# Attention scores on 64x64 quarters of TensorE, with new ranks, in an attention and mixture-of-experts kernel

## The chip, the cores and the metric

The kernel runs on one core of a Trainium2 chip, in one launch. The metric is the device time of the whole launch in microseconds; less is better. TensorE multiplies, VectorE, ScalarE and GpSimd do the rest, and SyncE issues most transfers. A product on TensorE reads both operands from SBUF and writes PSUM, which has eight banks of 128 partitions x 512 float32.

## The reference

Attention over 8 batches, 8 heads, 576 positions and 64 numbers a head, causal with a window of 128 keys and a bias by distance; then a mixture of 8 experts, of which each of the 4608 tokens takes two.

```python
scores = scale * np.matmul(q, k.transpose(0, 1, 3, 2))
bias = slopes[:, None, None] * (-np.abs(rel).astype(np.float32))[None, :, :]
mask = (rel >= 0) & (rel < window)                       # window = 128
scores = np.where(mask, scores + bias[None], -1000000000.0)
attn = softmax(scores)                                   # written out in full in the source
x = np.matmul(attn, v)                                   # to rows of 512 = 8 heads x 64
logits = x @ w_gate
noisy_logits = logits + np.log1p(np.exp(x @ w_noise)) * noise
top2 = np.argpartition(-noisy_logits, 2, axis=1)[:, :2]  # softmax weights over the two
for e in range(8):
    for k in range(2):
        mask = top2[:, k] == e
        h = np.maximum(x[mask] @ w1[e], 0.0)             # 512 -> 1024
        out[mask] += top2_w[mask, k, None] * (h @ w2[e]) # 1024 -> 512
```

## The kernel before

**Pairs and groups.** Work of attention goes by pairs of heads: 32 pairs (8 batches x 4), `k` in the code. One tile `qk` holds a pair: head 0 on partitions 0 to 63, head 1 on 64 to 127; in its columns the queries (`QW` = 640: 512, then the last 64 of head 0 and of head 1 side by side, with zeros on the other head's partitions) and then the 576 keys. The 576 queries are five blocks, four of 128 and one of 64. A `unit` is a pair and one of three groups of blocks: (0, 1), (2, 3), and the last block alone, which two pairs share; that is 80 units.

**A unit's stages.** `scores` (L498) multiplies a block of 128 queries with its 128 or 256 keys, for each head on its own 64 rows of the array, into that head's PSUM bank `s[h]`; `scores_of_last` (L513) does the last block of one pair, both heads in one full product with 192 keys, into `s[z]` for pair `z` of two. VectorE brings the 128 keys of each query's window together (`copy_predicated`, L524 and L532), adds the bias and takes the largest (L516); ScalarE takes the exponential (L540, L546); TensorE transposes (L553); ScalarE or VectorE copies the result out of PSUM (`evac`, L267 or L271); GpSimd cuts it at the diagonal (L573, L574); TensorE multiplies with the values (`weigh` L589, `weigh_last` L598) on two column halves. `rows`, `row_major` (L734, L737) and `gate` (L759, four strips of 32 columns; L770, L775) make token rows and gate logits of a batch, `route(b)` chooses the experts and writes the list of tokens (L875 and others).

**The experts.** Three blocks of expert 0 (384, 384 and 256 tokens, from the first 4, 6 and 7 batches) can start while attention runs; all others come in a second wave. `ups` (L1272) and `downs` (L1316, L1321) are float16 products in three passes, of weights and tokens split into a high and a low half (L1208 and L1244 make the low halves).

**What sets the order.** The program writes out its instructions in the order of a planner that runs at build time (class `Order`). Each piece of work is a coroutine that asks for an engine with a cost in microseconds and a rank (`pe`, `act`, `dve`, `pool`, `move`; `either` may go to ScalarE or VectorE, with an extra rank for VectorE). An engine that is free takes the ready piece of the lowest rank; TensorE prefers, within `NEAR` ranks, a piece of the same array mode (`like`) and is charged `SWITCH` where the mode changes. Ranks are the position `t` in the list of units plus constants: `STAGE` for the stages of a unit, `GATE`, `ROUTE`, `SCATTER` for a batch, `FFN0`, `FFN1`, `WEIGHTS`, `TOKENS`, `SIZES` for the experts, `LATE` for the engine choice. Costs and ranks only set the order; on the chip every engine runs its list in order and waits on semaphores. Tiles go round in rings (`qkr` 5, `pr` 5, `ptr` 4, two pairs of banks for scores in `sb`, two banks each in `tb` and `ob`).

Of the kernel before, what the change touches and what calls it, by code (L numbers as in the profile page):

```python
# [18 lines left out]
B, H, S, D = 8, 8, 576, 64  # L19
N, DM, E, F = B * S, H * D, 8, 1024  # L20
W = 128
NQ = 5
NP = H // 2
QW = 512 + 128
GROUPS = ((0, 1), (2, 3), (4,))
NF = 1
FIRST = ((0, 384, 4), (384, 384, 6), (768, 256, 7))
# [10 lines left out]
NTR = 512  # L38
NPAD = N + NTR
BLOCKS = tuple(((FROWS, c - FROWS),) if z < NF else ((0, 512), (512, 384), (896, c - 896)) for z, c in enumerate(CAPS))  # L40
ZERO, EMPTY = 61.9, -14
LOAD = -47.8
VALUES = 56.6
GATE = (-11.1, 47.4, 137.6, -25.3)
ROUTE = (1.0, 14.0, 40.1, 47.7)
SCATTER = (60.8, -1065.1, -1061.7, -1053.1, -38.3)
FFN0, FFN1 = 165.6, 267.3
WEIGHTS = (94.7, 86.4)
TOKENS = 101.2
STAGE = (-8.0, 5.7, 9.8, -7.2, -2.2, 32.3, 14.3, -20.1)  # L50
MIDDLE = 101.0
RESULT = -68.3
SIZES = (71.1, 72.1, 977.3)
SOON = 22.3
TIGHT = (1, 5, 7)
QUICK = (5, 7)
LATE = (-6.5, -40.7, 45.4, 103.9, -13.4, -112.7, 32.0, -155.9, 105.8, -25.4, 51.6, -29.7)
LAG = 0.2
TURN, MARGIN, LATE_BY = (1.4, 0.3), 1.0, 1.0
PACE, READ_BY, AHEAD = 4.0, 2.0, 16  # L60
HELD = 3
# [166 lines left out]
def attention_moe(ctx: ExitStack, tc: tile.TileContext, qk_, v, w_gate, w_noise, noise, w1, w2,  # L228
                  out, xs, slots, eye):
    nc = tc.nc  # L230
# [5 lines left out]
    bank = [psum.tile([128, 512], F32, name=f"bank{i}") for i in range(8)]  # L236
# [5 lines left out]
    order = Order()  # L242
# [5 lines left out]
    def pe(us, rank, emit, join=True, mode="full"):  # L248
        return Op((("PE", us, rank),), emit, join, mode)
# [51 lines left out]
    rel4, relc4 = scratch[1][:, 0:W], scratch[1][:, W:2 * W]  # L301
# [39 lines left out]
    def slope(h):  # L341
        return -8.0 * 2.0 ** -(h + 1)

    def masks():
        def window(out_, rel_):

            nc.vector.tensor_scalar(out_, rel_, 0.0, float(W), op0=OP.is_lt, op1=OP.mult)
            nc.vector.tensor_add(out_, out_, rel_)

        def full():  # L350
            nc.vector.tensor_scalar(own_key, rel, 0.0, None, op0=OP.is_ge)
            window(rel2[:, 0], rel)
            nc.vector.tensor_scalar(rel2[:, 1], rel, 0.0, 2.0 ** 40, op0=OP.is_lt, op1=OP.mult)
            nc.vector.tensor_add(rel2[:, 1], rel2[:, 1], rel)

        def halves():
            nc.vector.tensor_scalar(own_key4, rel4[:, 0:64], 0.0, None, op0=OP.is_ge)
            window(relc4, rel4)

        def bias_of(e, h):  # L360
            copy(e, bias[:, :, h], rel2, scale=slope(h))
            part = slice(h % 2 * 64, h % 2 * 64 + 64)
            copy(e, bias4[part, h // 2], relc4[part], scale=slope(h))

        yield dve(0.14, -40, lambda: nc.vector.tensor_scalar(ident, rel, 0.0, None, op0=OP.is_equal))
        yield dve(0.14, -40, lambda: nc.vector.tensor_scalar(before, rel, 0.0, None, op0=OP.is_lt))
        yield dve(1.0, -40, full)
        yield dve(0.6, -40, halves)
        for g in range(NP):
            for h in (2 * g, 2 * g + 1):  # L370
                yield either(0.56, 0.37, -20 + 5 * g, LATE[9], lambda e, h=h: bias_of(e, h))
            mark(biased[g])
# [118 lines left out]
    def scores(k, blocks, s):  # L491
        qk = qks[k]
        for z, i in enumerate(blocks):
            k0, c = (i - 1) * 128 if i else 0, width(i)
            o = place_of(blocks, z)
            for h in range(2):
                half = slice(h * D, h * D + D)
                nc.tensor.matmul(s[h][:, o:o + c], qk[half, i * 128:i * 128 + 128], qk[half, QW + k0:QW + k0 + c],  # L498
                                 start=True, stop=True)

    def width(i):
        return (128, 256, 256, 256, 192)[i]
# [7 lines left out]
    def scores_of_last(k, s):  # L510
        for z in range(2):
            qk = qks[k + z]
            nc.tensor.matmul(s[z][:, 0:192], qk[:, 512:QW], qk[:, QW + S - 192:QW + S], start=True, stop=True)  # L513

    def biased_and_largest(o, i, by, m):
        nc.vector.tensor_tensor_reduce(out=o, in0=i, in1=by, scale=-0.125, scalar=3.0e38, op0=OP.add, op1=OP.min, accum_out=m)  # L516
# [11 lines left out]
                biased_and_largest(p[:, z, h], s[h][:, o:o + W], bias[:, int(i == 0), 2 * g + h], nm[:, z, h:h + 1])  # L528

    def top_of_last(k, s, p, nm):  # L530
        for z in range(2):
            nc.vector.copy_predicated(s[z][:, 0:64], own_key4.bitcast(U32), s[z][:, W:W + 64])  # L532
        for z in range(2):
            biased_and_largest(p[:, z, 0], s[z][:, 0:W], bias4[:, (k + z) % NP], nm[:, z, 0:1])

    def soft(g, blocks, p, nm, den):
        for z, i in enumerate(blocks):
# [3 lines left out]
                                     accum_out=den[:, i, 2 * g + h:2 * g + h + 1])  # L541

    def soft_of_last(g, p, nm, den):
        for z in range(2):
            pv = p[:, z, 0]
            nc.scalar.activation(pv, pv, AF.Exp, bias=nm[:, z, 0:1], scale=-1.0,  # L546
                                 accum_out=den[:, 0, 2 * g + 2 * z:2 * g + 2 * z + 1])

    def trans(p, t, nh):
        for z in range(2):  # L550
# [4 lines left out]
    def evac(e, blocks, t, pt):  # L555

        if blocks == (4,):
            copy(e, pt[:, :, 0], t[:, 0:2 * W].rearrange("p (z c) -> p z c", z=2))
        else:
            copy(e, pt[:, :, 0:2] if blocks[0] == 0 else pt[:, :, 0:4:2], t.rearrange("p (h z c) -> p h z c", h=2, z=2))  # L560

    def split(blocks, pt):

        if blocks == (4,):
            a, b = (pt[:, :, x].rearrange("p z (h c) -> p z h c", h=2) for x in (0, 1))
            pattern = [[0, 2], [0, 2], [1, 64]]
# [24 lines left out]
    def weigh_last(k, pt, o):  # L591

        t = values_[k // 2]
        for z in range(2):
            for at, kb in ((0, 3), (1, 4)):
                for h in range(2):
                    half, hh = slice(h * D, h * D + D), (2 * z + h) * D
                    nc.tensor.matmul(o[half, z * D:z * D + D], t[:, kb, hh:hh + D], pt[:, z, at, half], start=at == 0, stop=at == 1)  # L598

    over, attended, seated = Event(n + B + B * NQ), Event(PAIRS + PAIRS // 2), Event(n)  # L600
    stored = [Event(NQ) for _ in range(B)]
# [10 lines left out]
    def unit(u):  # L612
# [5 lines left out]
        if last:  # L618
# [4 lines left out]
        yield biased[g + last]  # L623
        s = yield (sb, r0)
        mark(seated)
        yield pe((0.77, 0.98, 0.53)[gr], r0, lambda: scores_of_last(k, s) if last else scores(k, blocks, s),
                 mode="full" if last else "rows")
        for z in range(k, k + 1 + last):
            left[z] -= 1
            if not left[z]:  # L630
# [63 lines left out]
    def rows(b, last, t):  # L694

        yield filled[b, last]
        blocks, den = ((0, 1, 2, 3), (4,))[last], dens[b, last]
        nr, nz = 64 if last else 128, len(blocks)
        rank = t - GATE[kind(b)]

        def sums():
            if last:
                nc.vector.tensor_scalar(den[0:64, 0, 1:H:2], den[64:128, 0, 0:H:2], 1e-9, None, op0=OP.add)
                nc.vector.tensor_scalar(den[0:64, 0, 0:H:2], den[0:64, 0, 0:H:2], 1e-9, None, op0=OP.add)
# [867 lines left out]
    steps = [(blk, f) for blk in first + second for f in range(8)]  # L1572
    ranks = ranks1 + [1000 + s for s in range(8 * len(second))]

    nc.gpsimd.memset(ones, 1.0)
    nc.gpsimd.memset(one, 1.0)
    nc.gpsimd.iota(rel, pattern=[[-1, W]], base=0, channel_multiplier=1, allow_small_or_imprecise_dtypes=True)
# [1 line left out]
        nc.gpsimd.iota(rel4[z * 64:z * 64 + 64], pattern=[[-1, W]], base=0, channel_multiplier=1,  # L1579
                       allow_small_or_imprecise_dtypes=True)  # L1580
    nothing = nc.gpsimd.to_reg(0.0)
    order.busy["POOL"], order.busy["DVE"], order.busy["ACT"] = 2.5, 1.5, 1.9
    order.at(2.5, lambda: order.dispatch("POOL"))
    order.at(1.5, lambda: order.dispatch("DVE"))
# [101 lines left out]
```

## Time and profile before

| what | value |
|---|---|
| time of the runs | 1040.87 us median of 3 (1038.19 to 1041.65) |
| span of the profiled execution, first to last instruction | 1039.9 us |
| mean granted TensorE clock | 0.990 of 2.4 GHz |
| busy: TensorE, its weight loads, VectorE, ScalarE, GpSimd | 1006.7, 613.2, 684.7, 440.4, 367.3 us |
| first expert matmul starts | 231.1 us |
| last matmul ends | about 1030 us |

The profile names its own time as the span; no separate time of that execution is given, so the span stands for it, 0.9 us below the median of the runs. PE is TensorE, PEld its weight loads, DVE VectorE, ACT ScalarE, POOL GpSimd, SP SyncE. Busy time is the union of an engine's instructions. A line L498 is that line of the kernel. In a row, `out<-in` names the tile written and the tiles read, without buffer numbers; `64*128 64x256` is a stationary tile of 64 rows and 128 columns with a moving tile of 64 rows and 256 columns. A float32 product appears as two records.

### The profile page before, as it was taken

What the parts mean: (1) busy time and instruction counts of PE and PEld (TensorE: products, weight loads), DVE (VectorE), ACT (ScalarE), POOL (GpSimd) and SP (SyncE); (2) the same over time, 40 slices, a digit from 0 to 9 for tenths busy, and PEclk for the clock granted to TensorE, in tenths of its full rate; (3) what the DMA queues carried; (4) which work ended last, traced back from release to release, by engine and by line L of the source; (5) the groups of instructions that cost most, each with busy time, mean ns of one, the idle gap of its engine ahead of it and who ended that gap; (6) DMA issues with size and microseconds to landing.
All of it is one profiled execution on the core that took longest, in us unless ns stands there. A gap on an engine that the chain in (4) does not pass through costs nothing. (4 is left out here: it accounts for less than half of the span.)

```text
span 1039.9 us, 20426 instructions
## 1 busy us (share of the span) xinstructions
PE 1006.7 (97%) x6952; PEld 613.2 (59%) x6952; DVE 684.7 (66%) x2410; ACT 440.4 (42%) x1218; POOL 367.3 (35%) x572
## 2 busy tenths in 40 slices
PE   8998999989999999999999999999999999999996
PEld 6776766656557645654574457456644754584454
DVE  8988999997756857744777566467636834773311
ACT  8976887762222524332342344134313421442211
POOL 4356686664633203331232233143203320332202
PEclk9999999989999999999999999999999999999998
DMA  9856989835399879893997489859957794864223
GB/s 345 297 173 209 310 306 307 291 72 142 59 251 188 203 200 177 134 207 107 182 205 173 73 175 187 203 78 171 208 156 106 152 189 153 172 132 68 37 24 49
DMA packets 193338, 178.61 MB, mean 172 GB/s; under 512 B 104080, under 2 KB 147376, under 8 KB 193232
## 3 DMA queue, kind: packets, MB, share of 16 engines
q1 hardware_dynamic: 175888, 138.35, 49.2%
q0 software_dynamic: 17344, 38.94, 23.9%
q8 instruction: 55, 0.90, 0.4%
q14 instruction: 51, 0.42, 0.1%
HBM read 117.29 MB, written 40.71 MB: 152 GB/s over the span
## 5 line engine op out<-in xcount | busy, mean ns | idle before, releaser
L1405 POOL DMA_INDIRECT out_dram<-yo,ix x69 | 110.4, 1600 | 497.5 <-ACT yo L267 448.3
L1292 ACT ACTIVATE hh<-bank 128x384 f16<-128x384 f32 (+9 forms) x192 | 92.9, 484 | 449.4 <-PE bank L1272 442.5
L1307 DVE SCALAR_TENSOR_TENSOR hl<-bank,hh 128x384 f16<-128x384 f32 (+9 forms) x200 | 108.8, 545 | 255.9 <-ACT hh L1292 255.0
L1316 PEld LDWEIGHTS <-hh 128*128 128x128 f16 (+1 forms) x944 | 92.2, 98 | 100.2
L1272 PE MATMUL bank<-xh,w1hb 128*128 128x512 f16 (+8 forms) x384 | 127.0, 331 | 0.4 <-DMA xh<-th 0.4
L1272 PE MATMUL bank<-xh,w1lb 128*128 128x512 f16 (+8 forms) x384 | 127.1, 331 | 0.0
L1272 PE MATMUL bank<-xl,w1hb 128*128 128x512 f16 (+8 forms) x384 | 126.9, 330 | 0.1
L1272 PEld LDWEIGHTS <-w1ha 128*128 128x128 f16 x832 | 80.5, 98 | 48.8
L1272 PEld LDWEIGHTS <-w1hb 128*128 128x128 f16 x768 | 75.3, 98 | 55.5 <-issue 2.3
L1272 PE MATMUL bank<-xh,w1ha 128*128 128x384 f16 (+8 forms) x320 | 102.0, 319 | 0.0
L1272 PE MATMUL bank<-xh,w1la 128*128 128x384 f16 (+8 forms) x320 | 102.0, 319 | 0.0
L1272 PE MATMUL bank<-xl,w1ha 128*128 128x384 f16 (+8 forms) x320 | 102.0, 319 | 0.0
L540 ACT ACTIVATE p<-p,nm 128x128 f32<-128x128 f32 x256 | 99.0, 392 | 5.6 <-DVE nm L516 5.6
L1316 PE MATMUL bank<-w2ha,hl 128*128 128x512 f16 x244 | 92.5, 379 | 0.3 <-DVE hl L1307 0.3
L1316 PE MATMUL bank<-w2ha,hh 128*128 128x512 f16 x244 | 92.5, 379 | 0.0
L1316 PE MATMUL bank<-w2la,hh 128*128 128x512 f16 x244 | 92.5, 379 | 0.0
L1316 PE MATMUL bank<-w2hb,hl 128*128 128x512 f16 x228 | 86.4, 379 | 0.7 <-DVE hl L1307 0.7
L1316 PE MATMUL bank<-w2hb,hh 128*128 128x512 f16 x228 | 86.4, 379 | 0.0
L1316 PE MATMUL bank<-w2lb,hh 128*128 128x512 f16 x228 | 86.4, 379 | 0.0
L1219 POOL DMA_INDIRECT xg<-xs_dram,ix x69 | 73.8, 1070 | 32.4 <-issue 14.8
L1316 PEld LDWEIGHTS <-hl 128*128 128x128 f16 x472 | 46.4, 98 | 57.5 <-DVE hl L1307 2.4
L498 PE MATMUL bank<-qk 64*128 64x256 f32 (+1 forms) x512 | 67.1, 385 | 7.0 <-DMA qk<-in_qk_dram 4.6
(250 smaller groups left out, 2036.3 us busy)
## 6 DMA issues: line engine op xcount, KB each, us to landing
raw<-in_w_dram SPq DMA_DIRECT2D x144, 256.0 KB, 4.8
mraw<-in_w_dram SPq DMA_DIRECT2D x56, 512.0 KB, 4.1
qk<-in_qk_dram SPq DMA_DIRECT2D x32, 608.0 KB, 5.3
vraw<-in_v_dram SPq DMA_DIRECT2D x16, 640.0 KB, 6.6
out_dram<-xg SPq DMA_DIRECT2D x10, 1024.0 KB, 7.6
xs_dram<-x SPq DMA_DIRECT2D x32, 256.0 KB, 5.4
xg<-xs_dram,ix POOLq DMA_INDIRECT x69, 5.8
xh<-th SPq DMA_TRANSPOSE x69, 6.0
```

The costliest lines, as they stand in the source:

```text
L498: nc.tensor.matmul(s[h][:, o:o + c], qk[half, i * 128:i * 128 + 128], qk[half, QW + k0:QW + k0 + c], start=True, stop=True)
L540: nc.scalar.activation(pv, pv, AF.Exp, bias=nm[:, z, h:h + 1], scale=-1.0, accum_out=den[:, i, 2 * g + h:2 * g + h + 1])
L1219: yield pool(1.04, rank, lambda: nc.gpsimd.indirect_dma_start(out=xg[0:r], out_offset=None, in_=xs[0:blk.rows], in_offset=bass.IndirectOff ...
L1272: nc.tensor.matmul(t[:, 0:blk.n], wp[:, c], x[:, c, 0:blk.n], start=c == 0 and z == 0, stop=c == 3 and z == 2)
L1292: nc.scalar.activation(o, i, AF.Relu)
L1307: yield dve(0.07 + c * 0.00104, rank - MIDDLE, lambda: nc.vector.scalar_tensor_tensor(hl[:, 0:c], t[:, 0:c], 0.0, hh[:, 0:c], op0=OP.max, ...
L1316: nc.tensor.matmul(blk.y[j][0:r], h[:, cs], wp, start=f == 0 and m == 0, stop=f == 7 and m == 2)
L1405: ins = nc.gpsimd.indirect_dma_start(out=out, out_offset=bass.IndirectOffsetOnAxis(ap=blk.ix[0:r, j:j + 1], axis=0), in_=t[0:r], in_offset ...
```

## The change

Scores are made for 64 queries at a time, each with the 192 keys that its window can reach (128 in block 0): rows of the array by head, columns by the half of the block. The last block does the same with the two pairs on the two column halves, and the following steps index by head instead of by pair. Queries of the last block are stored plainly (`QW` = 576). Four banks are set to zero at the start, since parts of them are now read by `copy_predicated` without having been written. The planner's costs for scores become 0.66, 0.77 and 0.43, their mode "quads", VectorE's start 2.5 us, and nearly all rank constants get other values.

```diff
-QW = 512 + 128
+QW = S
-GATE = (-11.1, 47.4, 137.6, -25.3)
-ROUTE = (1.0, 14.0, 40.1, 47.7)
-FFN0, FFN1 = 165.6, 267.3
-WEIGHTS = (94.7, 86.4)
-TOKENS = 101.2
-STAGE = (-8.0, 5.7, 9.8, -7.2, -2.2, 32.3, 14.3, -20.1)
-MIDDLE = 101.0
-SIZES = (71.1, 72.1, 977.3)
+GATE = (3.6, 59.5, 91.3, -25.6)
+ROUTE = (-17.1, -7.9, 129.9, 106.1)
+FFN0, FFN1 = 161.5, 235.3
+WEIGHTS = (179.3, 122.0)
+TOKENS = 83.5
+STAGE = (-12.5, 2.4, 10.2, -53.4, 5.6, 68.2, 8.9, -3.8)
+MIDDLE = 61.3
+SIZES = (68.8, 88.3, 1078.7)
...
-LATE = (-6.5, -40.7, 45.4, 103.9, -13.4, -112.7, 32.0, -155.9, 105.8, -25.4, 51.6, -29.7)
+LATE = (-82.9, 60.2, 46.7, 37.7, -63.9, -132.3, 13.5, -126.2, 68.1, -124.1, 52.9, 59.5)
-SWITCH, NEAR = 0.093, 7.0
+SWITCH, NEAR = 0.093, 5.4
...
-            for h in range(2):
-                half = slice(h * D, h * D + D)
-                nc.tensor.matmul(s[h][:, o:o + c], qk[half, i * 128:i * 128 + 128], qk[half, QW + k0:QW + k0 + c],
-                                 start=True, stop=True)
+            for a in (0, 64):
+                first_, c_ = (a, c - 64) if i else (0, c)
+                for h in range(2):
+                    half = slice(h * D, h * D + D)
+                    nc.tensor.matmul(s[h][a:a + 64, o + first_:o + first_ + c_], qk[half, i * 128 + a:i * 128 + a + 64],
+                                     qk[half, QW + k0 + first_:QW + k0 + first_ + c_], start=True, stop=True)
...
     def scores_of_last(k, s):
         for z in range(2):
             qk = qks[k + z]
-            nc.tensor.matmul(s[z][:, 0:192], qk[:, 512:QW], qk[:, QW + S - 192:QW + S], start=True, stop=True)
+            for h in range(2):
+                half = slice(h * D, h * D + D)
+                nc.tensor.matmul(s[h][z * 64:z * 64 + 64, 0:192], qk[half, 512:QW], qk[half, QW + S - 192:QW + S],
+                                 start=True, stop=True)
...
-        yield pe((0.77, 0.98, 0.53)[gr], r0, lambda: scores_of_last(k, s) if last else scores(k, blocks, s),
-                 mode="full" if last else "rows")
+        yield pe((0.66, 0.77, 0.43)[gr], r0, lambda: scores_of_last(k, s) if last else scores(k, blocks, s),
+                 mode="quads")
...
+    for t in bank[0:4]:
+        nc.vector.memset(t, 0.0)
...
-    order.busy["POOL"], order.busy["DVE"], order.busy["ACT"] = 2.5, 1.5, 1.9
+    order.busy["POOL"], order.busy["DVE"], order.busy["ACT"] = 2.5, 2.5, 1.9
...
-    qk[..., 0:512], qk[..., QW:] = q[..., 0:512], k
-    for h in range(2):
-        qk[:, h, :, 512 + 64 * h:512 + 64 * h + 64] = q[:, h, :, 512:]
+    qk[..., 0:QW], qk[..., QW:] = q, k
```

## Rows read from the trace of the kernel before

**Rows 1.** The page: busy time by engine and share; busy tenths in 40 slices

```profile
PE 1006.7 (97%) x6952; PEld 613.2 (59%) x6952; DVE 684.7 (66%) x2410; ACT 440.4 (42%) x1218; POOL 367.3 (35%) x572
...
DVE  8988999997756857744777566467636834773311
```

**Rows 2.** Busy time by stretches, us: each engine, granted clock, DMA share, GB/s

```profile
26.00:52.00 26.00, 26.00 (x264) 19.80 (x262) 25.51 (x135) 25.36 (x111) 10.16 (x22) 1.00 0.88 297
...
104.00:156.00 52.00, 49.57 (x532) 35.64 (x534) 50.03 (x273) 43.47 (x174) 37.49 (x77) 1.00 0.90 308
...
208.00:231.10 23.10, 18.51 (x164) 12.85 (x163) 21.89 (x107) 15.44 (x57) 16.51 (x26) 0.85 0.40 81
231.10:1030.10 799.00, 793.85 (x4789) 458.40 (x4787) 471.12 (x1276) 254.77 (x464) 224.41 (x268) 1.00 0.73 148
26.00:231.10 205.10, 191.68 (x1993) 138.87 (x1992) 192.30 (x1014) 161.65 (x660) 129.46 (x261) 0.98 0.77 249
```

**Rows 3.** Waits until 231.1 us: us in total, times, longest

```profile
PE bank L498 <- DMA qk<-in_qk_dram: 4.6, 1, 4.6
...
DVE bank L524 <- PE bank L498: 3.7, 4, 2.6
```

**Rows 4.** TensorE's groups by form, 0 to 235 us: busy, mean ns, idle before

```profile
L498 PE MATMUL bank<-qk 64*128 64x256 f32 x384 | 57.1, 402 | 0.5 <-DVE nm L516 0.4
...
L498 PE MATMUL bank<-qk 64*128 64x128 f32 x128 | 17.1, 333 | 6.5 <-DMA qk<-in_qk_dram 4.6 <-DVE nm L516 1.8
```

**Rows 5.** Lines L498, L513 and L598: ns min/median/max, first and last start, forms

```profile
L498 PE MATMUL bank<-qk x512: 269/376/631, 4.6 to 227.5; 64*128 64x256 f32 x128, 64*128 64x128 f32 x43
...
L513 PE MATMUL bank<-qk x64: 326/326/430, 11.0 to 228.8; 128*128 128x192 f32 x64
...
L598 PE MATMUL bank<-pT,vraw x256: 219/222/270, 24.3 to 246.9; 128*64 128x64 f32 x128
```

**Rows 6.** TensorE's timeline, 60 to 66 us: start, length, line, count

```profile
61.17 0.69 PE L598 MATMUL bank<-pT,vraw 128*64 128x64 f32 x16
...
62.81 1.13 PE L498 MATMUL bank<-qk 64*128 64x256 f32 x8
63.87 0.66 PE L553 MATMUL bank<-ident,p 128*128 128x128 f32 x4
64.46 1.06 PE L759 MATMUL bank<-xu,wgn 128*32 128x512 f32 x8
```

**Rows 7.** VectorE's groups by form until 231.1 us: busy, mean ns, idle before

```profile
L516 DVE CUSTOM_DVE_ANT_0 p<-bank,bias 128x128 f32<-128x128 f32 x288 | 67.1, 283 | 0.1
L524 DVE COPY_PREDICATED bank<-own_key,bank 128x256 f32<-128x256 uint32 x64 | 24.0, 418 | 0.3 <-PE bank L498 0.2
L516 DVE DVE_READ_ACCUMULATOR2_ANT nm<- 128x1 f32 x288 | 23.1, 80 | 0.0
...
L524 DVE COPY_PREDICATED bank<-own_key,bank 128x128 f32<-128x128 uint32 x64 | 15.4, 284 | 3.5 <-PE bank L498 3.5
L271 DVE COPY xu<-bank 128x512 f32<-128x512 f32 x10 | 6.9, 687 | 2.4 <-PE bank L589 2.2
...
L271 DVE COPY pT<-bank 128x512 f32<-128x512 f32 x8 | 5.5, 685 | 0.3 <-POOL pT L574 0.2
```

**Rows 8.** Timelines of VectorE and TensorE, 3.5 to 6.3 us

```profile
6.24 0.30 DVE L524 COPY_PREDICATED bank<-own_key,bank 128x128 f32<-128x128 uint32 x1 [2.65 <-PE bank L498]
...
4.56 2.08 PE L498 MATMUL bank<-qk 64*128 64x128 f32 x10 [4.56 <-DMA qk<-in_qk_dram]
```

**Rows 9.** TensorE's timeline, 205 to 262 us: start, length, line, idle before

```profile
205.43 1.74 PE L589 MATMUL bank<-pT,vraw 128*64 128x256 f32 x20
...
213.06 0.55 PE L875 MATMUL bank<-hot,hot 128*80 128x64 f16 x10 [3.01 <-DVE gw L1235]
213.54 3.25 PE L589 MATMUL bank<-pT,vraw 128*64 128x256 f32 x20
```

**Rows 10.** The page's DMA issues: KB each, us to landing

```profile
qk<-in_qk_dram SPq DMA_DIRECT2D x32, 608.0 KB, 5.3
```

More of the change, by code (lines that the diff above doesn't have):

```diff
@@ L40 @@
 BLOCKS = tuple(((FROWS, c - FROWS),) if z < NF else ((0, 512), (512, 384), (896, c - 896)) for z, c in enumerate(CAPS))
-ZERO, EMPTY = 61.9, -14
-LOAD = -47.8
-VALUES = 56.6
-GATE = (-11.1, 47.4, 137.6, -25.3)
-ROUTE = (1.0, 14.0, 40.1, 47.7)
-SCATTER = (60.8, -1065.1, -1061.7, -1053.1, -38.3)
-FFN0, FFN1 = 165.6, 267.3
-WEIGHTS = (94.7, 86.4)
-TOKENS = 101.2
-STAGE = (-8.0, 5.7, 9.8, -7.2, -2.2, 32.3, 14.3, -20.1)
-MIDDLE = 101.0
-RESULT = -68.3
-SIZES = (71.1, 72.1, 977.3)
-SOON = 22.3
+ZERO, EMPTY = 53.9, -14
+LOAD = -139.5
+VALUES = 37.8
+GATE = (3.6, 59.5, 91.3, -25.6)
+ROUTE = (-17.1, -7.9, 129.9, 106.1)
+SCATTER = (105.4, -953.0, -1016.9, -1064.0, -103.8)
+FFN0, FFN1 = 161.5, 235.3
[3 more added lines that the diff above has]
+MIDDLE = 61.3
+RESULT = -57.8
+SIZES = (68.8, 88.3, 1078.7)
+SOON = -40.3
 TIGHT = (1, 5, 7)
 QUICK = (5, 7)
-LATE = (-6.5, -40.7, 45.4, 103.9, -13.4, -112.7, 32.0, -155.9, 105.8, -25.4, 51.6, -29.7)
+LATE = (-82.9, 60.2, 46.7, 37.7, -63.9, -132.3, 13.5, -126.2, 68.1, -124.1, 52.9, 59.5)
 LAG = 0.2
@@ L361, in bias_of @@
             copy(e, bias[:, :, h], rel2, scale=slope(h))
-            part = slice(h % 2 * 64, h % 2 * 64 + 64)
-            copy(e, bias4[part, h // 2], relc4[part], scale=slope(h))
+            part = slice(h // 2 % 2 * 64, h // 2 % 2 * 64 + 64)
+            copy(e, bias4[part, h // 4 * 2 + h % 2], relc4[part], scale=slope(h))
         yield dve(0.14, -40, lambda: nc.vector.tensor_scalar(ident, rel, 0.0, None, op0=OP.is_equal))
@@ L530, in top_of_last @@
     def top_of_last(k, s, p, nm):
[L531 to L534, printed above, removed]
+        for h in range(2):
+            nc.vector.copy_predicated(s[h][:, 0:64], own_key4.bitcast(U32), s[h][:, W:W + 64])
+        for h in range(2):
+            biased_and_largest(p[:, h, 0], s[h][:, 0:W], bias4[:, k % NP + h], nm[:, h, 0:1])
     def soft(g, blocks, p, nm, den):
@@ L543, in soft_of_last @@
     def soft_of_last(g, p, nm, den):
[L544 to L547, printed above, removed]
+        for h in range(2):
+            pv = p[:, h, 0]
+            nc.scalar.activation(pv, pv, AF.Exp, bias=nm[:, h, 0:1], scale=-1.0,
+                                 accum_out=den[:, 0, 2 * g + h:2 * g + h + 1])
     def trans(p, t, nh):
@@ L557, in evac @@
         if blocks == (4,):
-            copy(e, pt[:, :, 0], t[:, 0:2 * W].rearrange("p (z c) -> p z c", z=2))
+            copy(e, pt[:, :, 0], t[:, 0:2 * W].rearrange("p (h c) -> p h c", h=2))
         else:
@@ L564, in split @@
         if blocks == (4,):
-            a, b = (pt[:, :, x].rearrange("p z (h c) -> p z h c", h=2) for x in (0, 1))
+            a, b = (pt[:, :, x].rearrange("p h (z c) -> p h z c", z=2) for x in (0, 1))
             pattern = [[0, 2], [0, 2], [1, 64]]
@@ L597, in weigh_last @@
                     half, hh = slice(h * D, h * D + D), (2 * z + h) * D
-                    nc.tensor.matmul(o[half, z * D:z * D + D], t[:, kb, hh:hh + D], pt[:, z, at, half], start=at == 0, stop=at == 1)
+                    nc.tensor.matmul(o[half, z * D:z * D + D], t[:, kb, hh:hh + D], pt[:, h, at, z * D:z * D + D], start=at == 0, stop=at == 1)
     over, attended, seated = Event(n + B + B * NQ), Event(PAIRS + PAIRS // 2), Event(n)
@@ L702, in sums @@
             if last:
-                nc.vector.tensor_scalar(den[0:64, 0, 1:H:2], den[64:128, 0, 0:H:2], 1e-9, None, op0=OP.add)
-                nc.vector.tensor_scalar(den[0:64, 0, 0:H:2], den[0:64, 0, 0:H:2], 1e-9, None, op0=OP.add)
+                lower, upper = (den[z:z + 64, 0].rearrange("p (a b) -> p a b", b=4) for z in (0, 64))
+                nc.vector.tensor_scalar(lower[:, :, 2:4], upper[:, :, 0:2], 1e-9, None, op0=OP.add)
+                nc.vector.tensor_scalar(lower[:, :, 0:2], lower[:, :, 0:2], 1e-9, None, op0=OP.add)
             else:
@@ L1581, in attention_moe @@
     nothing = nc.gpsimd.to_reg(0.0)
-    order.busy["POOL"], order.busy["DVE"], order.busy["ACT"] = 2.5, 1.5, 1.9
+    order.busy["POOL"], order.busy["DVE"], order.busy["ACT"] = 2.5, 2.5, 1.9
     order.at(2.5, lambda: order.dispatch("POOL"))
-    order.at(1.5, lambda: order.dispatch("DVE"))
+    order.at(2.5, lambda: order.dispatch("DVE"))
     order.at(1.9, lambda: order.dispatch("ACT"))
```

## Prediction

> **What bounds the kernel now.** I read the page first, then the busy time by stretches, then the waits, then the two engines that are full, by form.
>
> The page alone misleads: TensorE is busy for 97% of the span and VectorE for 66% [rows 1], which looks like a kernel with one bound. The strip of slices shows that VectorE's 66% is a mean of two stages: nearly full in the first 22% of the span, half idle later. The stretches cut it there [rows 2]. Until 231.1 us the program is attention and routing, with no matmul of the experts; from 231.1 to 1030.1 it is the expert matmuls, TensorE busy 793.85 of 799.00 us. What comes after 231.1 is therefore a sequence that TensorE sets alone: it moves as a whole when its start moves, and the reader should ask only what sets that start.
>
> Between 26 and 231.1 us two engines are full at once: TensorE 191.68 of 205.10 us, VectorE 192.30. From 26 to 52 both are almost without a gap (26.00 and 25.51 of 26). ScalarE has 43 us free. Transfers have a high share too, but TensorE waited for one only once in this stage, 4.6 us for the very first queries and keys [rows 3]. A score group is written by TensorE, then read by VectorE (L524, L516), and both queues are in order, so a gap on the one soon becomes a gap on the other. The change makes work shorter on TensorE alone.
>
> **The change part by part.**
>
> *The scores.* A score record has 192 columns (L513) at 326 ns, 256 (L498, median) at 376 and 128 (L498, least) at 269 [rows 5]. 128 more columns cost 107 ns, or 0.836 ns a column; a float32 product has two records. Two heads run side by side. So before, one group of blocks 0 and 1 streams 2 x 128 + 2 x 256 = 768 columns per head, 0.642 us; one of blocks 2 and 3 streams 1024, 0.856 us; a last group passes four records of 192 one after another, 768 columns, 0.642 us. The trace has the middle one from 62.81 to the next work at 63.87, 1.06 us [rows 6]: 0.86 of stream and 0.20 around it. After, if all four quarters stream at once, each carries 640, 768 and 384 columns: 0.535, 0.642 and 0.321 us. The saving is 0.107, 0.214 and 0.321 us. There are 32, 32 and 16 such groups (128 and 384 records of the two L498 forms [rows 4], 64 of L513 [rows 5]): 3.4 + 6.9 + 5.1 = 15.4 us.
>
> Do four stream at once? The trace has no record with half the rows and half the columns. Two nearest rows: four 32-column strips of a float32 product (L759) finish eight records of 512 columns, that is 8 x 0.43 = 3.4 us of stream, in 1.06 us; two column halves (L598) finish 16 records of 64 in 0.69 us [rows 6]. Rows in halves are L498 itself. I take four; the other end is two at a time, 1.070, 1.284 and 0.642 us, which makes the scores 32 x 0.428 + 32 x 0.428 = 27.4 us longer. The saving is gone below 2.9 quarters at once (42.7 x 4 / 58.2).
>
> Records double, from 576 to 1152. L598 gives 31 ns for each ((0.69 - 0.222) / 15), so 16 records take 0.50 us of issue, under 0.535 and 0.642. It does not bind, narrowly in blocks 0 and 1. The far row is L589, 20 records in 1.74 us [rows 9], 72 ns each, though there columns set the pace: 1152 x 0.072 = 82.9 us against 58.2.
>
> A rule speaks against this step. The Trainium skill, "TensorE: Matmul & The Clock Gate", section "Wait — 56ns, not 53.3ns?", says that with the hardware decoder off the sequencer spends about 62 ns on each matmul, which then binds when the array work is shorter. By it the scores would take an estimated 1152 x 0.062 = 71.4 us, 13 more than before, where L598's row makes them 15.4 less. The 31 ns of L598 say that this case is not under that rule.
>
> *The last group changes its mode.* It was a full-array product among full-array transposes; it now opens and closes a tiled stretch like the others. Bounds: nothing, where it lies beside other quarters, up to the 0.20 us seen around a group, 16 x 0.20 = 3.2 us. I take half, 1.6. TensorE then saves 13.8 us (12.2 to 15.4).
>
> *VectorE's part.* copy_predicated, the biased maximum and the sums keep their counts and sizes: L516 and L524 alone are 129.6 us of this stage [rows 7]. Four memsets of 128 x 512 in PSUM are added. No row has one; the ends are nothing and the 687 ns of a 128 x 512 copy from PSUM, 0 to 2.7 us. They lie before VectorE's first score at 6.24 us, where it sat idle for 2.65 us, and TensorE starts only with its first transfer at 4.56 [rows 8]. I cost them at nothing; without that cover they cost up to 2.7.
>
> *The input.* The query-key transfer shrinks from 608 KB [rows 10] to 576, nobody waits for it after the first: nothing. Softmax, transposes and sums of the last group keep their sizes: nothing.
>
> *The ranks.* They move nothing in amount. They decide which ready work TensorE, VectorE and the DMA queues take, and whether the `either` copies fall to ScalarE. They can lose by a wait at the head of a queue. The price of one is shown at 210 to 213 us: L875 stood 3.01 us for VectorE, and the next L589 group took 3.25 us [rows 9] where the same 20 records took 1.74 at 205, since the granted clock had fallen (0.85 as the mean of that stretch, a mix of the levels 1.2 and 2.4 GHz [rows 2]). That is 4.5 us for one wait.
>
> **The sum.** From 26 to 231.1 TensorE's need falls by 13.8 us, VectorE's does not. VectorE can hardly be fuller than from 26 to 52: 25.51 / 26 = 98.1%. Its 192.30 us then take 196.0 us instead of 205.1: the start of the expert matmuls moves 9.1 us forward. The rest of TensorE's saving, 4.7 us, becomes gaps. Ends: nothing gained, if VectorE keeps its 93.8%; 13.8, if copies leave VectorE (L271's two forms of 128 x 512 are 12.4 us [rows 7]) for ScalarE. Profiled span 1039.9 us; the median of the runs, 1040.87, lies 0.9 above it, and what lies around the span stays. 1040.9 - 9.1 = 1031.8, rounded to 1032.
>
> **The rivals.**
>
> *All of it passes through* (15 in 100). ScalarE takes the copies, and TensorE stays the bound: 1040.9 - 13.8 = 1027, 1025.5 with the full 15.4. For it: ScalarE's free time. Against it: VectorE's 98% from 26 to 52 with ScalarE busy there too, 25.36 of 26.
>
> *VectorE keeps the start where it is* (15 in 100). Its gaps come from route chains and from buffers, not from the scores: of its waits only 3.7 us are for L498, 2.6 of these the first one [rows 3]. Then TensorE's 13.8 us turn into idle time: 1038 to 1041. This is what the Trainium skill would say, "TensorEngine Tiling (Array Packing)", section "PSUM Bottleneck": a faster TensorE does not speed the emptying of PSUM, which may bind in its place. By that rule no gain; the trace agrees in so far as VectorE is at 94%.
>
> *Quarters don't run four at once* (2 in 100). Two at a time: 1040.9 + 27.4 = 1068. It ends slower from below 2.9 on.
>
> *Issue binds* (3 in 100). At L589's 72 ns a record: 1040.9 + 24.7 = 1066; slower from 50 ns on (58.2 / 1152). The sequencer rule above would give 1054 by its estimate.
>
> *The new order adds waits* (10 in 100). A wait as at 210 us costs 4.5 us. TensorE has more gaps to fall into when VectorE binds, and each may halve the clock behind it. From three more on, 13.5 us, the 9.1 are gone; four make it 1050 with nothing hidden. Against it: each shorter score leaves slack of which such a wait first eats.
>
> **How the numbers follow.** Forecast 55 in 100: its own range is 1029 to 1036. Faster by over 0.3% (below 1037.7; 0.3% is about what three runs, 1038.2 to 1041.7, can tell from no change): 55 + 15 = 0.70. Within: 0.15. Slower: 2 + 3 + 10 = 0.15. The range goes from 1025, the full saving, to 1042, the unmoved start with the memsets uncovered; the three slow cases lie outside it.
>
> **What would show it.** Score records of 192 columns, four starting together, a group of blocks 2 and 3 in some 0.8 to 0.85 us to the next work; the first expert matmul near 222 us; VectorE above 96% from 26 us to there, TensorE below its present 93.5%; the stretch behind it still about 799 us. It is wrong if the first expert matmul stays near 231, if the tail stretch grows by more than 3 us (the ranks then cost expert matmuls), or if the score groups keep 1.06 us.

## The result and the profile after

The changed kernel takes 1027.51 us (median of 4 runs, 1026.49 to 1030.66), the kernel before, measured beside it, 1039.53. The ratio is 0.9877, 95% interval 0.9853 to 0.9902: some 12.8 us less. That lies in the range of 1025 to 1042, but not in the forecast's own range of 1029 to 1036: it is the figure of the rival in which all of TensorE's saving passes through (1027).

The profiled execution has a span of 1024.8 us. First its busy time by stretches; the columns are those of [rows 2]. The first row ends at the first expert matmul, the second at the first matmul of the second wave (the experts after the three early blocks of expert 0), the third at the last matmul.

```profile
0.00:210.30 210.30, 197.56 (x2738) 138.03 (x2739) 198.81 (x1102) 184.30 (x759) 131.66 (x295) 0.99 0.82 273
210.30:314.30 104.00, 99.63 (x693) 58.00 (x691) 82.48 (x266) 31.58 (x67) 49.22 (x73) 0.98 0.70 159
314.30:1014.60 700.30, 695.97 (x4102) 399.12 (x4100) 402.73 (x1037) 226.09 (x404) 179.69 (x203) 1.00 0.71 147
26.00:210.30 184.30, 176.43 (x2460) 123.81 (x2460) 175.62 (x974) 161.73 (x667) 121.87 (x256) 0.99 0.80 265
```

The same three stretches of the kernel before, cut at its own events:

```profile
0.00:231.10 231.10, 212.81 (x2165) 154.83 (x2166) 213.55 (x1136) 184.95 (x753) 140.76 (x303) 0.98 0.79 260
231.10:328.60 97.50, 97.20 (x688) 58.50 (x687) 68.93 (x240) 28.32 (x61) 41.11 (x64) 1.00 0.72 155
328.60:1030.10 701.50, 696.65 (x4102) 399.90 (x4100) 402.19 (x1036) 226.45 (x404) 183.30 (x204) 1.00 0.73 147
```

The reader is to see three things. The first expert matmul starts 20.8 us earlier (231.1 to 210.3), far more than forecast. The stretch behind it gives 6.5 back (97.5 to 104.0): TensorE stands idle 4.4 us there instead of 0.3, and VectorE has 82.5 us to do in it instead of 68.9. The second wave, 700 us long, is nearly the same. Net: 15.5 us to the last matmul between these two executions, 12.8 by the ratio.

Of the 6.5 us, 2.4 are TensorE's own busy time (97.20 to 99.63, at a granted clock of 0.98 instead of 1.00). Of its 4.4 us of idle time, half is one wait for GpSimd's part of a batch's list of tokens; in the kernel before, the same product (L875 there) waited 3.01 us in front of the start [rows 9].

```profile
213.57 0.54 PE L881 MATMUL bank<-hot,hot 128*80 128x64 f16 x10 [2.17 <-POOL hot L877]
```

Between 26 us and the first expert matmul, both engines lost about the same amount: TensorE 191.68 to 176.43, VectorE 192.30 to 175.62 [rows 2]. The second number is the surprise, since the new scores leave VectorE's work as it was. Its rows say what left. VectorE's weight preparation in the first stretch, before and after (columns as in [rows 7]; before):

```profile
L1208 DVE SCALAR_TENSOR_TENSOR w1la<-raw,wsc,w1ha 128x512 f16<-128x512 f32 x7 | 5.6, 805 | 0.0
L1208 DVE SCALAR_TENSOR_TENSOR w2la<-raw,wsc,w2ha 128x512 f16<-128x512 f32 x7 | 5.4, 772 | 0.0
L269 DVE TENSOR_SCALAR w2ha<-raw,wsc 128x512 f16<-128x512 f32 x2 | 1.6, 808 | 0.0
...
L269 DVE TENSOR_SCALAR w1ha<-raw,wsc 128x512 f16<-128x512 f32 x1 | 0.7, 676 | 0.0
```

after, with the memsets:

```profile
L1214 DVE SCALAR_TENSOR_TENSOR w1la<-raw,wsc,w1ha 128x512 f16<-128x512 f32 x3 | 2.3, 764 | 0.0
L1582 DVE MEMSET bank<- 128x512 f32 x4 | 1.9, 485 | 1.1 <-PEq L1681 1.0
L1214 DVE SCALAR_TENSOR_TENSOR w2la<-raw,wsc,w2ha 128x512 f16<-128x512 f32 x2 | 1.4, 695 | 0.0
```

13.3 us of expert 0's weights before, 3.7 after: 9.6 us now come behind the first expert matmul. The rest of what left is mostly copies out of PSUM (L271, 3.4 us) and the making of a batch's list (`hot`, L866 before and L872 after, 2.7 us). The constant WEIGHTS suggests itself as the cause of the 9.6 us, but e3 and e12 below speak against that.

The scores themselves, by line (as [rows 5]) and in TensorE's timeline (as [rows 6]):

```profile
L500 PE MATMUL bank<-qk x1024: 269/322/579, 4.7 to 204.7; 64*64 64x192 f32 x128, 64*64 64x128 f32 x43
```
```profile
L517 PE MATMUL bank<-qk x128: 322/323/374, 11.0 to 205.8; 64*64 64x192 f32 x128
```
```profile
60.05 0.94 PE L500 MATMUL bank<-qk 64*64 64x192 f32 x16
60.92 0.55 PE L558 MATMUL bank<-ident,p 128*128 128x128 f32 x3
```

A group of blocks 2 and 3 with its 16 records occupies 60.05 to 60.92, 0.87 us, where it was 1.06. Had the quarters run one or two at a time, 16 records of 192 columns would need 1.28 us or more (worked out from the 0.836 ns a column of the prediction). TensorE's busy time over the span fell from 1006.7 to 993.2 us, 13.5.

The start, on VectorE:

```profile
0.98 2.11 DVE L1582 MEMSET bank<- 128x512 f32 x4 [0.98 <-PEq L1681]
...
6.09 0.49 DVE L529 COPY_PREDICATED bank<-own_key,bank 128x128 f32<-128x128 uint32 x2 [1.12 <-PE bank L500]
```

Four memsets take 2.1 us and lie wholly in the idle time before the first score, which VectorE reads at 6.09 us (6.24 before [rows 8]).

### The profile page after: what moved, and what is told of

Same layout as the page of the kernel before. It is cut to its first block, busy times and chain, and to the rows that moved or that the text cites. A ratio compares the mean times of both kernels' runs of the same rounds, so it can differ in the third digit from the quotient of the medians.

```text
span 1024.8 us, 21575 instructions
## 1 busy us (share of the span) xinstructions
PE 993.2 (97%) x7528; PEld 595.2 (58%) x7528; DVE 684.0 (67%) x2403; ACT 442.7 (43%) x1229; POOL 362.7 (35%) x572
## 5 line engine op out<-in xcount | busy, mean ns | idle before, releaser
L1298 ACT ACTIVATE hh<-bank 128x384 f16<-128x384 f32 (+9 forms) x188 | 90.8, 483 | 433.4 <-PE bank L1278 400.6
L1322 PEld LDWEIGHTS <-hh 128*128 128x128 f16 (+1 forms) x944 | 92.1, 98 | 101.6 <-ACT hh L1298 2.0
L1322 PE MATMUL bank<-w2ha,hh 128*128 128x512 f16 x244 | 92.5, 379 | 1.0 <-ACT hh L1298 1.0
L1322 PE MATMUL bank<-w2ha,hl 128*128 128x512 f16 x244 | 92.5, 379 | 0.7 <-DVE fit L486 0.6
L1322 PE MATMUL bank<-w2la,hh 128*128 128x512 f16 x244 | 92.5, 379 | 0.0
L1322 PE MATMUL bank<-w2hb,hl 128*128 128x512 f16 x228 | 86.4, 379 | 0.3 <-DVE hl L1313 0.3
L1322 PE MATMUL bank<-w2hb,hh 128*128 128x512 f16 x228 | 86.5, 379 | 0.1
L1322 PE MATMUL bank<-w2lb,hh 128*128 128x512 f16 x228 | 86.4, 379 | 0.0
L1225 POOL DMA_INDIRECT xg<-xs_dram,ix x69 | 70.2, 1018 | 36.0 <-issue 21.4
L1322 PEld LDWEIGHTS <-hl 128*128 128x128 f16 x472 | 46.4, 98 | 58.8 <-DVE hl L1313 2.9
L267 ACT ACTIVATE th<-xg,fit 128x512 f16<-128x512 f32 (+5 forms) x75 | 53.5, 717 | 36.4 <-DVE fit L1238 31.2
```

What stands on the lines that cost most here:

```text
L1225: yield pool(1.04, rank, lambda: nc.gpsimd.indirect_dma_start(out=xg[0:r], out_offset=None, in_=xs[0:blk.rows], in_offset=bass.IndirectOff ...
L1298: nc.scalar.activation(o, i, AF.Relu)
L1322: nc.tensor.matmul(blk.y[j][0:r], h[:, cs], wp, start=f == 0 and m == 0, stop=f == 7 and m == 2)
```

## The experiments

Two theories stood first. **A**: the gain is TensorE's shorter work alone; VectorE could follow; the ranks hardly matter. **B**: VectorE would have held the gain near 9 us, as the prediction had it, and the new ranks lifted that by putting off work. All twelve runs compare with the kernel before as it ran beside them; its median there was 1042.27 us (for e1, e2, e3 and e7), 1042.21 (for e4, e5, e6 and e8) and 1040.70 (for e9 to e12), so ratios are to be compared, not times. "Start" is the first expert matmul, "stretch" from there to the second wave, both in us from the profiled execution.

| run | median us | ratio to before, 95% interval | start | stretch | second wave |
|---|---|---|---|---|---|
| kernel before | 1039.53 | 1 | 231.1 | 97.5 | 701.5 |
| changed kernel | 1027.51 | 0.9877 (0.9853 to 0.9902) | 210.3 | 104.0 | 700.3 |
| e1 quarters, old ranks | 1046.60 | 1.0036 (1.0015 to 1.0056) | 223.8 | 110.6 | 704.0 |
| e2 old scores, new ranks | 1048.37 | 1.0054 (1.0035 to 1.0073) | 230.7 | 108.8 | 700.1 |
| e3 old WEIGHTS alone | 1050.81 | 1.0080 (1.0057 to 1.0102) | 218.3 | 116.0 | 700.2 |
| e4 more work on VectorE | 1048.01 | 1.0063 (1.0040 to 1.0085) | 229.5 | 107.7 | 701.0 |
| e5 more work on TensorE | 1042.93 | 1.0010 (0.9994 to 1.0026) | 222.4 | 104.6 | 698.7 |
| e6 last block in full | 1034.99 | 0.9922 (0.9909 to 0.9935) | 212.8 | 112.5 | 705.0 |
| e7 halves in turn | 1029.29 | 0.9876 (0.9851 to 0.9901) | 210.5 | 106.7 | 700.3 |
| e8 all scores as before, order kept | 1042.69 | 1.0013 (0.9994 to 1.0031) | 219.7 | 109.8 | 701.5 |
| e9 e1 with late fit | 1054.58 | 1.0127 (1.0104 to 1.0150) | 226.9 | 93.4 | 723.0 |
| e10 e3 with late fit | 1065.05 | 1.0226 (1.0205 to 1.0247) | 227.0 | 109.9 | 720.1 |
| e11 changed kernel with late fit | 1048.66 | 1.0078 (1.0053 to 1.0103) | 222.7 | 101.5 | 714.1 |
| e12 e1 with new WEIGHTS | 1038.98 | 0.9976 (0.9957 to 0.9995) | 220.9 | 104.2 | 704.2 |

Executions of one kernel spread by up to 11 us (e5, 1037.6 to 1048.8), and the one profiled can lie off its median: those of e3 and e5 by some 5 us below, that of e6 by 7 above. A column of the table is one execution; the ratio is the verdict.

### The quarters alone: e8, e6 and e7

e8 keeps the program of the changed kernel, every piece of work in the same place, and makes the scores as before. The edit of e8:

```diff
-            for a in (0, 64):
-                first_, c_ = (a, c - 64) if i else (0, c)
-                for h in range(2):
...
+            for h in range(2):
+                half = slice(h * D, h * D + D)
+                nc.tensor.matmul(s[h][:, o:o + c], qk[half, i * 128:i * 128 + 128], qk[half, QW + k0:QW + k0 + c],
+                                 start=True, stop=True)
```

(and `scores_of_last` with its indexing, and the layout of the queries, as before). e6 does this for the last block only. By their traces VectorE, ScalarE and GpSimd run the same operations in the same sequence in e5 to e8 as in the changed kernel.

> The changed kernel with all scores as before (two row halves, 128 queries with 256 keys; last block in full), in the order that the planner made for the quarters: the quarters alone, undone. Theory A: 12 to 15 us longer, 1039 to 1043, the old time. Theory B: the part that the ranks give stays, 4 to 9 us longer, 1031 to 1037.

> The changed kernel with the last block's scores as before, one full product for each pair, and the indexing that goes with it; the order of all work stays that of the changed kernel. TensorE has 16 x 0.321 = 5.1 us more stream, less up to 3.2 for mode changes that go. Theory A: 2 to 5 us longer, 1029 to 1033. Theory B: 0 to 2 us longer.

e8 is 0.0136 above the changed kernel's ratio, 14.1 us of 1040 (each of the two ratios is known to about 2 us); e6 0.0045, 4.7 us. By size both are theory A's figures: TensorE's saved time was 13.8 us in the sum and 3.5 for the last block (5.1 less half of the mode changes). Where it lands is clear only up to the start: until then TensorE is busy for 207.81 us in e8 and 197.56 in the changed kernel, 10.2 more, and the start comes 9.4 later (219.7 against 210.3). Another 5.8 us of e8's profile are in the stretch, which has no scores. e7, as fast as the changed kernel and in the same order, has 2.7 of these too, so part of them is a matter of the single execution.

Read against the kernel before, e8 shows what the new order does alone: same scores, other order. The rows are from 26 us to the start and the stretch:

```profile
26.00:219.70 193.70, 187.67 (x2006) 136.50 (x2005) 179.09 (x978) 162.99 (x667) 121.18 (x256) 1.00 0.79 256
219.70:329.50 109.80, 101.40 (x693) 58.13 (x691) 82.46 (x266) 31.54 (x67) 48.61 (x73) 0.97 0.67 151
```

The start is 11.4 us earlier than before and VectorE has 13.2 us less to do in front of it (192.30 to 179.09), the stretch is 12.3 us longer, and the time is that of the kernel before (1.0013, interval 0.9994 to 1.0031). So what the new order puts off, it pays back; in that order the quarters are the whole gain.

e7 issues the same matmuls in another order inside a group:

```diff
-        for z, i in enumerate(blocks):
...
-            for a in (0, 64):
+        for a in (0, 64):
+            for z, i in enumerate(blocks):
...
```

> The changed kernel with the score matmuls in another order: the lower half of both blocks first, then the upper half; the same matmuls, the same place of each group in the program. If TensorE starts matmuls in program order, two quarters at a time work and a group of blocks 2 and 3 takes about 1.1 instead of 0.64 us of stream: 64 groups x 0.45 = 27 us more of TensorE's time. Theory A: 1045 to 1055 us. Theory B: part of it falls in TensorE's idle time, 1035 to 1048 us. If the queue overlaps the halves anyway: 1027 us.

Its ratio is that of the changed kernel. A group takes 60.23 to 61.09, 0.86 us, as if nothing had changed (TensorE's timeline of e7):

```profile
60.23 0.93 PE L500 MATMUL bank<-qk 64*64 64x192 f32 x16
61.09 0.66 PE L558 MATMUL bank<-ident,p 128*128 128x128 f32 x4
```

In program order the lower quarters have all their eight records before the first of the upper ones. Started strictly in that order, the upper four slots could overlap only the last of the lower, seven slots of 0.16 us, 1.1 us. So a quarter need not wait for what stands before it in the program on another quarter. (The records do not name their quarter; this rests on the order of the program and the 0.86 us.)

### Which engine sets the start: e4 and e5

Both add work that changes no result and leave the order alone.

```diff
-                biased_and_largest(p[:, z, h], s[h][:, o:o + W], bias[:, int(i == 0), 2 * g + h], nm[:, z, h:h + 1])
+                for again in range(1 + (z == 0 and h == 0)):
+                    biased_and_largest(p[:, z, h], s[h][:, o:o + W], bias[:, int(i == 0), 2 * g + h], nm[:, z, h:h + 1])
```

(e4; in the last group one of two, too) and

```diff
-            for a in (0, 64):
+            for a in (0, 64) * (2 - z):
```

(e5).

> The changed kernel with one biased maximum (L521) of each of the 80 units made twice: 80 x 0.212 = 17.0 us more for VectorE until the scores are done, on TensorE nothing; same order. Theory A (TensorE sets the end): 0 to 6 us longer, 1027 to 1034. Theory B (VectorE sets it): 12 to 17 us longer, 1039 to 1045.

> The changed kernel with the scores of the first block of each of 64 groups made twice: 32 x 0.214 + 32 x 0.321 = 17.1 us more for TensorE, on VectorE nothing; same order. Theory A: 14 to 17 us longer, 1041 to 1045. Theory B: TensorE's idle time takes most of it, 0 to 7 us longer, 1027 to 1035.

e4 is 19.3 us above the changed kernel, e5 13.8. What was added is not quite what was worked out: over the span VectorE is busy for 704.9 us in e4 instead of 684.0, 20.9 more and not 17.0, and TensorE for 1006.1 in e5 instead of 993.2, 12.9 more and not 17.1. Nearly all of the one and all of the other lands. So both theories fail: A cannot have VectorE's work land, B cannot have TensorE's. The stretches from 26 us to the start show why (e4, then e5; columns as above):

```profile
26.00:229.50 203.50, 185.50 (x2509) 128.05 (x2508) 197.34 (x1129) 166.53 (x672) 120.79 (x257) 0.98 0.76 243
```
```profile
26.00:222.40 196.40, 189.61 (x2927) 138.04 (x2924) 179.29 (x979) 163.18 (x667) 122.28 (x255) 1.00 0.77 251
```

With more work, VectorE fills 97.0% (TensorE 91.2%); with more on the other side, TensorE fills 96.5% (VectorE 91.3%). In the changed kernel they stand at 95.3% and 95.7%: both within two points of the most that either reached, so extra work on either moves the start. In the kernel before it was 93.8% and 93.5%.

### The ranks: e1, e2, e3 and e12

e1 puts all rank constants of the kernel before into the changed one, e2 all new ones into the kernel before, e3 and e12 move one constant:

```diff
-WEIGHTS = (179.3, 122.0)
+WEIGHTS = (94.7, 86.4)
```

(e3, on the changed kernel; e12 the reverse, on e1).

> The quarters of the changed kernel with every rank constant of the kernel before (the planner's costs for scores stay new). Theory A: the gain is TensorE's shorter work alone (13.5 us less busy time), VectorE could follow, the ranks hardly matter: 1026 to 1030 us. Theory B: VectorE would have held the gain to about 9 us, and the new ranks lifted that by putting off the preparation of expert 0's weights and some copies: 1031 to 1036 us, first expert matmul near 222 us.

> The kernel before with every rank constant of the changed kernel, scores and their costs as before. Theory A: no change, 1037 to 1042 us. Theory B: VectorE has some 14 us less to do before the first expert matmul, which comes earlier than 231 us, but TensorE's work is unchanged: 1034 to 1039 us.

> The changed kernel with the one constant WEIGHTS set back from (179.3, 122.0) to (94.7, 86.4), so that expert 0's weights are prepared early again. Theory A: 1026 to 1029 us. Theory B: VectorE has some 9.6 us more before the first expert matmul, which comes 5 to 10 us later than 210 us; 1031 to 1036 us.

> e1 with the one constant WEIGHTS of the changed kernel. If putting off expert 0's weights is what frees VectorE before the first expert matmul, that comes 5 to 10 us before e1's 223.8 us, at 214 to 219. The time then depends on the stretch behind it: 1036 to 1042 without a wait at the head of VectorE's queue, up to 1050 with one.

e1 is 3.7 us slower than the kernel before, outside what either theory gave. Its start, 223.8, is nearly the 222 that the prediction and theory B name, but the stretch behind it takes 110.6. By the busy time of e1:

```profile
223.80:334.40 110.60, 100.54 (x689) 58.48 (x686) 75.74 (x252) 30.82 (x72) 44.04 (x68) 0.97 0.65 145
334.40:1038.40 704.00, 698.23 (x4108) 400.00 (x4106) 401.19 (x1035) 227.02 (x403) 184.67 (x203) 1.00 0.72 146
26.00:223.80 197.80, 181.04 (x2460) 125.69 (x2461) 187.46 (x998) 160.37 (x655) 130.99 (x261) 0.98 0.78 253
```

TensorE stands idle for 10.1 us of the stretch. e2 is slower than the kernel before too (5.6 us), where both theories had it the same or faster: its start hardly moves (230.7), its stretch takes 108.8. So with the order planned anew, neither the quarters with all old ranks nor the new ranks with the old scores gain; together they gain 1.2%.

e3 tells what one constant does: 21.1 us above the changed kernel. Its start is 8.0 us later (theory B's 5 to 10), with VectorE's work before it at 205.62 instead of 198.81 us. But that is not the weight preparation of which theory B spoke. VectorE's rows of it in e3, until the start:

```profile
L1214 DVE SCALAR_TENSOR_TENSOR w1la<-raw,wsc,w1ha 128x512 f16<-128x512 f32 x3 | 2.8, 923 | 0.0
L1214 DVE SCALAR_TENSOR_TENSOR w2la<-raw,wsc,w2ha 128x512 f16<-128x512 f32 x2 | 1.6, 776 | 0.0
L269 DVE TENSOR_SCALAR w1ha<-raw,wsc 128x512 f16<-128x512 f32 x1 | 0.6, 555 | 0.0
```

They are 5.0 us, 1.3 more than in the changed kernel; most of the 6.8 us are lists (`hot`, L872: 12.6 instead of 8.7) and copies (L271, 1.3 more). e12 agrees: with the new WEIGHTS 9.2 us of preparation come before the start, with the old one, in e1, 8.2. So WEIGHTS acts through the order that comes out as a whole, and not by bringing expert 0's weights forward or putting them off.

e3's stretch is 12.0 us longer, which neither theory had. The stretch, its TensorE, then its VectorE in the middle of it:

```profile
218.30:334.30 116.00, 100.78 (x685) 58.70 (x685) 79.38 (x258) 31.48 (x72) 41.77 (x66) 0.94 0.60 145
```
```profile
303.81 0.38 PE L1322 MATMUL bank<-w2ha,hh 128*128 128x512 f16 x1
304.03 0.38 PE L1322 MATMUL bank<-w2la,hh 128*128 128x512 f16 x1
314.62 0.61 PE L1322 MATMUL bank<-w2ha,hl 128*128 128x512 f16 x1 [10.21 <-DVE hl L1313]
```
```profile
307.17 0.16 DVE L1023 SCALAR_TENSOR_TENSOR ix<-list,ix 128x3 int32<-128x3 f32 x1
312.46 0.69 DVE L1246 TENSOR_REDUCE fit<-xg 128x1 f32<-128x512 f32 x1 [5.12 <-DMA xg<-xs_dram,ix]
...
314.06 0.16 DVE L1244 TENSOR_REDUCE gw<-xg 128x1 f32<-128x8 f32 x1
314.14 0.41 DVE L1313 SCALAR_TENSOR_TENSOR hl<-bank,hh 128x256 f16<-128x256 f32 x1
```

TensorE waits 10.21 us for `hl`, 0.41 us of VectorE's work. VectorE could not make it: the maximum of a tile of tokens (L1246) stood ahead of it in the list and waited 5.12 us, with VectorE idle, for the gather of these tokens (from 304.4, when TensorE's wait began, to 307.3 VectorE had other work of its list to do). After the wait the records of TensorE are 0.61 us where they were 0.38: the granted clock had fallen, to 0.94 as the mean of the stretch. e1 has two such places (3.3 and 3.8 us before L1322; in the second VectorE did two more operations between the gather and `hl`). In e2, VectorE stood 6.55 us for a transfer of weights (L1177) and TensorE 6.18 us for `hl`.

What such a wait costs changes from one execution to the next. e6 has the order of the changed kernel; at one and the same place of it, VectorE waited in the changed kernel, then in e6:

```profile
303.81 0.69 DVE L1246 TENSOR_REDUCE fit<-xg 128x1 f32<-128x512 f32 x1 [1.33 <-DMA xg<-xs_dram,ix]
```
```profile
312.09 0.69 DVE L1242 TENSOR_REDUCE fit<-xg 128x1 f32<-128x512 f32 x1 [7.25 <-DMA xg<-xs_dram,ix]
```

TensorE's wait behind it was 0.6 and 6.1 us; that execution of e6 is the one 7 us above its median. So one profile tells that such a wait occurs, not its mean price.

e12, e1 with only the new WEIGHTS, is 6.2 us faster than e1 and 2.5 faster than the kernel before; but its start moves by 2.9 us, less than was expected, and 6.4 of the profiled difference are in the stretch (104.2). In both pairs (e3 and the changed kernel, e1 and e12) the constant moves the stretch more than the start.

### The wait at the head of VectorE's queue: e9, e10 and e11

**C**: the stretch is longer where VectorE stands for a gather with TensorE's `hl` behind it. **D**: VectorE simply has too much left to do there. The edit tells the planner that gathers land later:

```diff
-        yield max(order.now + 3.4, order.transfer(order.now, 2048.0 * r))
+        yield max(order.now + 3.4, order.transfer(order.now, 2048.0 * r)) + 5.0
```

> e1 (quarters with the old ranks), where the planner takes each gather of tokens to land 5 us later, so that VectorE's first instruction on them stands later in its queue. Theory C: in the stretch from the first expert matmul to the second wave TensorE starved because VectorE stood at the head of its queue for a gather, with the high-low split that TensorE needed behind it (3.3 and 3.8 us, and half clock after each). Then that stretch falls from 110.6 to 98 to 104 us, and the time from 1046.6 to 1033 to 1041. Theory D: VectorE simply has too much work left in that stretch: it stays at 108 to 112, the time within 3 us of e1's.

> e3 (the changed kernel with the old WEIGHTS) with the same 5 us. Theory C: the 10.2 us gap before L1322 and the 13.7 us of half clock go, the stretch falls from 116.0 to 100 to 106 us, the time from 1050.8 to 1035 to 1042; the first expert matmul stays near 218. Theory D: stretch 112 to 118, time within 3 us of e3's.

> The changed kernel with the same 5 us. Theory C: its stretch has only 4.4 us of TensorE idle time, of which 1.0 and 0.6 before L1322; 0 to 4 us can be had, 1025 to 1030, unless the new order brings a collision of its own. Theory D: no difference beyond 2 us.

In e9 the stretch falls further than C said:

```profile
226.90:320.30 93.40, 92.03 (x644) 54.56 (x642) 61.27 (x205) 23.43 (x52) 40.46 (x63) 1.00 0.61 150
320.30:1043.30 723.00, 705.74 (x4115) 400.79 (x4113) 413.89 (x1073) 227.51 (x405) 184.58 (x203) 1.00 0.65 144
```

93.4 us instead of 110.6, TensorE idle 1.4 instead of 10.1 and the granted clock full. But e9's stretch also holds less work than e1's (TensorE 644 records instead of 689, VectorE 61.27 us instead of 75.74), so D's cause, too much work, is not excluded. And every time came out worse, against the forecasts of both: the edit delays all gathers, those of the second wave too, and that grew by 19.0 us (idle 17.3 instead of 5.8). e10's stretch fell by 6.1 only, between the two forecasts, with new gaps of the same kind (9.7 us for `hl` in six places of the whole run), and its start moved to 227.0. e11 moved its start by 12.4 us, 5.2 of it one wait of L881 for VectorE. So e3's lines show the mechanism of C at one place; that it makes up the whole difference of the stretches is not shown, and as a remedy the edit fails. One that delays only the gathers of the stretch was not tried, and no version here beats the changed kernel.

## Why the prediction was right, and where it was wrong

*The scores.* Right. Four quarters stream at once, records of 192 columns take 322 ns (326 for the full array before), a group of blocks 2 and 3 occupies 0.87 us, just above the 0.80 to 0.85 named. TensorE's busy time fell by 13.5 us where the sum had 13.8 (by 12.5 from e8, with the order held), and e8 gives 14.1 us of time for it. Issue did not bind, with 16 records in 0.87 us.

*The last group.* Bounded at 2 to 5 us in all, 4.7 by e6.

*The memsets and the input.* Right: 2.1 us, inside the idle time; no wait for queries and keys later.

*The sum* failed at "TensorE's need falls by 13.8 us, VectorE's does not" and, under it, "They move nothing in amount", said of the ranks. They move no amount over the whole run, but across the very event on which the sum rests: 9.6 us of weight preparation, some copies and part of a list went behind the first expert matmul, and VectorE's need between 26 us and it fell by 16.7 us, 13.2 of them by the order alone (e8). So that start came at 210.3 instead of 222, with VectorE at 95.3%, under the 96% named, and TensorE up to 95.7% from 93.5, where it was to fall. The premise that the rest "moves as a whole when its start moves" failed with it: the stretch grew by 6.5 us, and in e8 by 12.3, about what the start had won. The text had named "if the tail stretch grows by more than 3 us" as a sign against it, and it did, by 5.3 with the second wave.

*The start with the ranks of before* is what the sum priced: 222.0 worked out, 223.8 in e1. That they agree is partly luck: the sum had VectorE at 98.1% with 192.30 us to do, and in e1 it is at 94.8% with 187.46; no run reached 98.1%. And the time of e1 was still 1046.6 because of its stretch.

*The range held* for a reason of which the sum had one half: the size of TensorE's saving. That all of it came through was priced as a rival, and an order that adds waits as another, of 10 in 100; e1 and e3, the same quarters in other orders, lie above 1042 us.

*TensorE's remaining 4.7 us "becomes gaps".* Not so: with the order held, 10.2 us less of TensorE's work moved the start by 9.4, and the time by 14.1 (how the part behind the start comes about is not shown). The ceiling of 98.1% was not the only bound to look at; e4 and e5 show two engines that both push the time, nearly one for one.

*The rivals.* "All of it passes through" came true in its figure, though not by the copies that ScalarE was to take: VectorE's copies of `xu` and `pT` (L271) before the start fell from 12.8 to 9.4 us, but they are the same in e8, which gains nothing. "VectorE keeps the start where it is" did not occur. The rule of the Trainium skill that stood beside it ("TensorEngine Tiling (Array Packing)", section "PSUM Bottleneck") holds in that emptying PSUM got no faster (284 and 418 ns a piece for L524, 284 and 417 for L529), and e4 shows VectorE near its limit, at 97.0%; but it did not bind in place of TensorE, which still passed its saving on. Two quarters at a time are excluded by the group's length. Nor is this case under the sequencer rule ("TensorE: Matmul & The Clock Gate" of the Trainium skill, section "Wait — 56ns, not 53.3ns?"): by its 62 ns 16 records would need an estimated 0.99 us, and they occupy 0.87. "The new order adds waits" did not befall the changed kernel, but e1, e2 and e3 show how near it was: e1 and e3 lie 16.5 and 21.1 us above the changed kernel, and a single wait was 10.2 us, not the 3.0 read at 210 us.

What stays open: why ranks set for one set of scores collide with the other is shown only at the places named. In the order of the changed kernel the quarters are worth about 14 us and the order itself nothing; what they would be worth in other orders as good as this one, no run here tells.

## What to carry to other kernels

When two engines are full and the order is planned, price a structural change with the order held (e8 against the changed kernel) and the new order with the old structure (e8 against the kernel before): here the first was the whole gain and the second nothing, while planning anew with one half of the change (e1, e2) was slower than before. Ask of a change of priorities what it moves across the event that sets the end, not only what it adds. And read the head of each in-order queue: an instruction that waits for a transfer with a 0.4 us step behind it that a full engine needs can cost nearly as much as the whole change brings (10.2 us in e3, 12.8 for the change).

## What the runs showed of the hardware

Float32 matmuls on the four 64 x 64 quarters ran at once, 16 records of 192 columns in 0.87 us with what lies around them, and they did so whether the program alternated the quarters or gave one half all its records first (0.86 us). The price of a wait was also more than its length: after the 10.2 us in e3, float16 records of 512 columns took 0.61 us instead of 0.38, and the granted clock was 0.94 as the mean of that stretch, a mix of the levels 1.2 and 2.4 GHz, where the kernel before had 1.00 in its own.
